# A fused recurrence and feed-forward kernel: spreading the first chunk's decays with four large matmuls per tile

## The chip, the cores and the metric

The kernel runs on one core of one Trainium2 chip. The metric is the device time of one execution in microseconds (us): the median of several runs. Engines are named as in the profile: PE (TensorE matmuls), PEld (its weight loads), DVE (VectorE), ACT (ScalarE), POOL (GpSimd), SP (SyncE, which issues all data transfers).

## What is computed

The reference, cut to what matters (B=4, H=8, S=768, D=40):

```python
for t in range(S):
    m_new = maximum(f[t] + m, i[t])
    f_stab, i_stab = exp(f[t] + m - m_new), exp(i[t] - m_new)
    C = f_stab * C + i_stab * outer(v[t], k[t])
    n = f_stab * n + i_stab * k[t]
    y[t] = sigmoid(o[t]) * (C @ q[t]) / maximum(abs(n @ q[t]), 1)
x = y.transpose(0, 2, 1, 3).reshape(B * S, H * D)        # 3072 x 320
h = x @ w_in                                             # 320 -> 2048
out = where(h > 0, h, exp(minimum(h, 0)) - 1) @ w_out    # 2048 -> 320
```

## The kernel before

**Tiles.** Time is cut into 6 chunks of 128 steps, and a tile is one chunk of one batch element with its 8 heads: 24 tiles, n = 4 x chunk + batch element. Inside a tile the recurrence is done in two halves of 64 steps: the state is carried from half to half, and within a half a 64x64 matrix per head holds the products of decays. The feed-forward part takes two tiles at a time (a block of 256 columns) and 16 slices of 128 of the 2048 inner features. While the weights are still arriving, the first blocks are done for some of the slices only, with partial sums stored and fetched back (`SPLITS`).

**Gates (`gate_chunk`, lines 355 to 392).** For each chunk the maximum m is a scan along time, the decays exp(f + m - m_new) go to `dec` (64 rows, one for each half, batch element and head, by 64 steps), and their running products to `cum`. Both are written to DRAM (`fstore`, line 381, and `bstore`, line 385).

**Decays spread over partitions.** A tile needs the decays of its 8 heads as rows that are the same on 64 partitions. `load` (line 394) fetches them back from DRAM with a source that repeats (`wdload` into `w`, line 416, and `bbload` into `bb`, line 425). For tiles 0 and 1 (`SPREAD_BY_PE`, line 181) PE does this instead: `spread` multiplies `dec` by one column of the identity, repeated 64 times, in 16 matmuls of 64 columns, and `spread_b` does the same for `cum` in 8. The result stays in PSUM, in the two banks `ph` for tile 0 and `pc` for tile 1, which the feed-forward part uses later.

**A tile's chain (`attention`, line 429).** On DVE the scan `ws` (line 478) turns the spread decays into the 64x64 matrices, and `kw` scales the keys by their last column. On PE come `kq` (line 496, products of keys and queries into the bank `pa`) and `us` (line 507, the sums for the state, also into `pa`). DVE multiplies `pa` into `w` (`wp`, line 522) and updates the state (`shrink`, `gather`). PE then forms the tile's output `y` in the bank `pb` (line 556): first state times queries (8 matmuls in the first chunk), then weights times values in 32 pieces, each 64 rows by 32 output partitions. DVE, ACT and POOL divide by the denominator and multiply by the gate (`den` to `result`), 64 columns are copied (`xdup`), PE transposes three blocks (`turn`, line 614, again into `pb`), and ACT and DVE split the result into a high and a low part (`xh`, `xl`), the feed-forward part's input. `pb` is one buffer, so the `y` of the next tile waits for `xl` of this one.

**Feed-forward (`ffn`).** Line 653 is the first layer (8 matmuls of 256 columns for one slice), lines 661 to 670 the nonlinearity and its split, line 680 the second layer (6 matmuls of 320 columns for one slice of a block).

**Weights (`conversion`, line 268).** They arrive as 64-bit words in 18 pieces (`wide`, line 285) and are turned into high and low parts by some eight steps on ACT, DVE and POOL.

**Order.** Every step is an `op` with a list of what it reads and writes. The table `PLACES` gives each step its place in one order of the whole program, and for some its engine (a letter behind the number). Each engine runs its steps in that order and waits for what a step needs; SP issues the transfers in that order too, and a transfer that must wait for its buffer holds those behind it.

Of the kernel before, what the change touches and what calls it, by code (L numbers as in the profile page):

```python
# [14 lines left out]
ALU = mybir.AluOpType  # L15
I32 = mybir.dt.int32
# [3 lines left out]
P = 128  # L20
# [6 lines left out]
    0 4 1 5 6v 3 35v 37 24 40 38 42 44 49 9 48 52 51 55 54 58 62 71 19 22 69 84 77 87 74 91 109 140 137 142 45 99  # L27
# [5 lines left out]
    775 2 10 14 17 13 21 20 15 23 26g 33 78 81 18 30a 12 11 8 39v 65 34 28 43 46 47 50 53 57 56 63 66 60 68v 70  # L33
    72g 76 80 85a 92 95 100 31 27 16 61 111 41 64 59 67g 83 88 94 96 93v 127 129 105 116 119 121g 124 126 128a 130
    133 138 7 25 29g 32 79 36 98 82 102 168g 170 173 178 143 145a 144 153 162 171 179 192 202 207 216 160 166 176
    183 222 228 233 241 245 256 262 251 255 90 86 89 75 73 101 97 135v 136 108 132 131 139 152g 151 146 149v 154
    158 161 163 165g 169 175 182a 184 187 191 113 114 112 107 110 115 117 164v 167 157 172 174 180 189g 185 190
    198v 227 197 210v 211 214 215 218 220a 221 224 226 229 235 243 247 257 264 277 283 307 260 266 274 278 285 298
    302 319 324 344 349 358 380 279 287 295 311 317 323 356 362 366 293 299 331 335 338 341 364 372 381 351 407
    412 365 411 527 330 340 360 363 382 398 406g 419 422 346 354 369 390 399 410 421 434 439 418 471 538 424 480  # L40
    615 203 193 181 188 186 199 195 246v 252 238 248 250 253 270 263 254v 267 291v 300 273 288 290 292g 294 297
    301a 305 310 313 236 232 217 208 213 237 240 296 303 281 286g 312 316 328 322 314 321 352 378 336 342v 343 345
    348 353 357a 361 371 375 122 194 209g 280 200 308 289 355 395 474 477 500 498 387 409a 396 402 428 430 433 438
    457 484 491 408 414 425 431 436 458 466g 497 502 445 449 465 469 473 481 499 512 517 462 467 476 511 516 521
    526 553 557 566 568 573 727 259 332 265 269 242 334 329 383 347 367 377g 389 393 417 403 397v 405 415v 446 429
    437 442 444g 447 448 451a 454 456 470 384 391 373 370 368 386 413 443v 435 427 440 455 459 460 463 452v 468
    478 513 472 486 488 492 494 496 508v 510 518 520 525 530 544 546 551 555 572 585 588 537 543 550 554 556 563
    569 594 602 560 564 587 591 599 605 610 619 623 570 576 596 601 606 612 629 646 652 667 767 670 832 607 614
    620 627 644 653 679 686 690 626 630 635 637 664 677 692g 707 714 658 663 689 693 695 698 713 756 760 671 680
    706 711 718 731g 753 780 785 748 805 836 781 813 815 722 729 737 740 759 774 779 819 828 735 741 757 758 764  # L50
    794g 798g 843 849 766 772 783 789 793 821 837 855 867 777 791 807 809 817 852 868 871 877 861 890 893 860 892
    990 799 804 847 851 876 880 885g 895 898 835 853 870 875 881 884v 888 903 910 883 886 889 899 901 908g 912g
    929 931 887 891 897 900 907 918v 920 934 938 894 942 944 902 949 1155 914 917 924 925 933 936 939g 964 986 922
    926 937 940 943 947v 950g 993 997 941 945 954 967 970 980 992g 1002 1023 951 958 965 969 987 1008 1016g 1031
    1042 1010 1045 1146 963 1047 1208 503 505 426 493 489 534 532 485v 487 539 545 547 549 613 583 577v 580 597v
    604 634 642v 647 649g 659 662 681a 684 687 691 595 593 581 584 524 598 542 632v 631 625 633 639 641 666g 669
    657v 674 676v 697 694 700 702 704 705 709 715a 721 725 728 376 450 475g 490g 464g 519 655 716 708 726 749 784
    788 734 736a 978 983 999 1003 1007 1012v 1026g 1049 1052 1006 1013 1018 1021 1024 1029g 1051 1055 1061 1017
    1019 1033 1038 1053 1057g 1060g 1067 1087 1036 1046 1054 1056 1059 1072g 1080 1092 1097 1062 1070 1078 1081
    1085 1094 1100g 1103 1107 1075 1083 1088 1091 1096 1099v 1108g 1120 1124 1101 1102 1104 1106 1109 1111 1114  # L60
    1132 1141 1110 1112 1116 1117 1119 1129g 1131g 1145 1153 1166 1168 1158 1372 611 617 540 578 574 603 645 683v
    682 621 660g 699 703 719g 733 710 723 730v 732 744 763v 768 769 770 773 787a 796 800 802 672 648 665 643 668
    717 678 738v 742 739 745 751 754 782 797 786v 790 792v 795 811 820 824 827 829 834 838a 841 845 848 1115 1118
    1122 1123 1125 1165v 1167 1174 1178 1126 1130 1135 1137 1140 1148 1157g 1181 1184 1156 1159 1171 1177 1180
    1183g 1185 1211 1219 1164 1169 1175 1179 1192 1196 1215 1223 1227 1187 1191 1201 1206 1225 1229v 1232g 1239
    1249 1205 1230 1234 1236 1238 1241g 1244g 1253 1255 1233 1237 1240 1242 1245 1247 1254 1264 1268 1243 1246
    1250 1252 1256 1258v 1259g 1270 1273 1279v 1303 1276 1446 724 720 712 762 765 801 803 778v 776 808 812 810 816
    846g 850 833 840 844 856 859 864 865 866 869 873 878 882 896 961 826 818 831 806 822 911 913 858v 906 854 857
    862 863 966 953 927 930 932v 956 974 979 981 982 984 985 988a 991 994 996 675 814 823 825g 872 830 904 874 935
    1063g 1065 1014 1011 1001 1004a 1257 1260 1262 1265 1267 1277v 1280g 1289 1292 1261 1269 1271 1272 1274 1278  # L70
    1284g 1306 1331 1275 1281 1285 1293 1295 1304 1316g 1333 1337 1283 1286 1290 1291 1296 1311 1335g 1347 1350
    1312 1319 1326 1329 1332 1336 1352 1376 1379 1325 1339 1344 1346 1349 1357 1367g 1393 1398 1343 1353 1355 1356
    1359 1377g 1382 1400 1403 1364 1369 1375 1378 1380 1391 1401 1407 1410 1434v 1455 1430v 1458 842 919 923 909
# [79 lines left out]
def tile_mlstm_then_elu_ffn(  # L153
# [634 lines left out]
```

## Time and profile before

| | before |
|---|---|
| median of 3 runs | 479.54 us (479.01 to 480.01) |
| the profiled execution's own time | 480.55 us |
| its span | 478.8 us |
| PE busy | 448.0 us, 94% of the span |
| DVE, ACT, POOL busy | 294.7, 229.0, 145.4 us |
| moved by DMA | 51.31 MB, 107 GB/s over the span |
| instructions that DMA brings in (queue q8) | 51 packets, 0.84 MB |

The span is the time between the first and the last instruction of the profiled execution; its own time is 1.75 us longer. Busy shares are sums over the whole span. Matmuls overlap, so PE's busy share says that it had something under way, not that it ran at its peak. In the trace, one float32 matmul of the program is two records on PE, a transpose or a float32r matmul is one.

### The profile page before, as it was taken

The page shows a single profiled execution, that of the slowest core. Times are in us where ns is not written, and L with a number is a line of the kernel's source. Part 1 is how long each engine was busy: PE and PEld are TensorE (multiplying, and loading weights), DVE is VectorE, ACT ScalarE, POOL GpSimd, SP SyncE. Part 2 cuts the span into 40 slices and gives each one's busy share as a digit, 9 for nine tenths or more (in the row PEclk, how much of TensorE's full clock was granted, in tenths as well). Part 3 has the DMA queues.
Part 4 walks back from the last instruction along what each step waited for, and adds up shares of the span by engine and source line. Part 5 has one row for each costly group of instructions (what it writes and reads, how often), then busy time and mean ns, then how long its engine had stood idle before and what let it go on. Part 6 is the DMA issues. An engine that isn't in the chain of part 4 may idle for free.

```text
span 478.8 us, 15219 instructions
## 1 busy us (share of the span) xinstructions
PE 448.0 (94%) x6574; PEld 435.6 (91%) x6574; DVE 294.7 (62%) x556; ACT 229.0 (48%) x440; POOL 145.4 (30%) x164
## 2 busy tenths in 40 slices
PE   4568999989799989999999999999999999999997
PEld 3557899979799989999999999999999999999996
DVE  6588899969959974767457425565663353353422
ACT  4466698669746432442533344333532334333443
POOL 2243235513432223433242543121223231222131
PEclk9998899989979999999999999999999999999999
DMA  7796967587944365620723304207050000010000
GB/s 220 174 256 186 249 189 194 128 231 197 258 111 114 95 162 125 171 77 15 168 65 98 107 2 129 85 12 207 0 137 7 0 16 1 1 44 1 27 1 27
DMA packets 23892, 51.31 MB, mean 107 GB/s; under 512 B 4794, under 2 KB 11130, under 8 KB 23826
## 3 DMA queue, kind: packets, MB, share of 16 engines
q1 hardware_dynamic: 23826, 50.35, 39.4%
q8 instruction: 51, 0.84, 0.8%
q14 instruction: 15, 0.12, 0.1%
HBM read 44.24 MB, written 6.09 MB: 105 GB/s over the span
## 4 chain that ended last, share of the span: by engine, by line
PE 84%; DMA 3%; issue 3%; DVE 2%; POOL 1%; ACT 1%; SPq 1%; POOLq 0%; DVEq 0%
PE ph L653 36%; PE pc L680 35%; PE pb L556 6%; PE pa L496 3%; PE pa L507 2%; DMA qk<-in_qk 2%; PE pb L614 2%; DMA wide<-in_w_in 1%; DVE vko L594 0%; POOL xf L199 0%; DVE xl L619 0%; SPq L416 0%; POOL qk L520 0%; DVE w L522 0%; POOL den L592 0%
## 5 line engine op out<-in xcount | busy, mean ns | idle before, releaser
L653 PE MATMUL ph<-xh,w 128*128 128x256 f32 x960 | 186.3, 286 | 0.6 <-ACT xh L617 0.6
L680 PE MATMUL pc<-w,gh 128*128 128x320 f32 x768 | 177.8, 319 | 0.3 <-issue 0.3
L653 PEld LDWEIGHTS ph<-xh,w 128*128 128x128 f32 x960 | 148.6, 191 | 1.6 <-ACT xh L617 1.0
L680 PEld LDWEIGHTS pc<-w,gh 128*128 128x128 f32 x768 | 130.2, 194 | 1.4 <-issue 0.4
L665 DVE SCALAR_TENSOR_TENSOR e<-e,ph 128x512 f32<-128x512 f32 (+1 forms) x97 | 65.3, 677 | 101.8 <-ACT e L663 99.7
L653 PE MATMUL ph<-xl,w 128*128 128x256 f32 x576 | 124.0, 284 | 0.2 <-DVE xl L619 0.2
L680 PE MATMUL pc<-w,gl 128*128 128x320 f32 x384 | 121.2, 316 | 0.0
L661 ACT ACTIVATE e<-ph 128x512 f32<-128x512 f32 (+1 forms) x97 | 57.4, 593 | 133.1 <-PE ph L653 103.1
L653 PEld LDWEIGHTS ph<-xl,w 128*128 128x128 f32 x576 | 96.4, 191 | 0.4 <-DVE xl L619 0.4
L670 POOL TENSOR_TENSOR gl<-e,gh 128x512 fp32r<-128x512 f32 (+1 forms) x44 | 57.6, 1309 | 124.0 <-ACT gh L199 70.4
L680 PEld LDWEIGHTS pc<-w,gl 128*128 128x128 f32 x384 | 74.4, 194 | 0.0
L663 ACT ACTIVATE e<-e 128x512 f32<-128x512 f32 (+1 forms) x97 | 60.3, 627 | 2.3
L322 POOL TENSOR_TENSOR narrow<-narrow,wide 128x512 int32<-128x512 int32 (+1 forms) x18 | 27.5, 1529 | 59.4 <-issue 14.9
L670 DVE TENSOR_TENSOR gl<-e,gh 128x512 fp32r<-128x512 f32 (+1 forms) x53 | 38.1, 720 | 11.1 <-PE pc L680 6.5
L199 ACT CAST gh<-e 128x512 fp32r<-128x512 f32 (+1 forms) x52 | 31.5, 607 | 19.0 <-DVE e L665 18.3
L199 POOL CAST gh<-e 128x512 fp32r<-128x512 f32 x20 | 13.7, 687 | 49.4 <-DVE e L665 49.4
L478 DVE TENSOR_TENSOR_SCAN w<-w,ones 128x512 f32<-128x512 f32 x22 | 27.1, 1234 | 0.7 <-DMA w<-f_d 0.7
L556 PE MATMUL pb<-va,w 64*32 64x41 f32 x1536 | 21.3, 207 | 3.9 <-issue 3.9
L617 ACT CAST xh<-pb 128x384 fp32r<-128x384 f32 x24 | 11.4, 475 | 25.6 <-PE pb L614 24.3
L507 PE MATMUL pa<-va,vko 64*64 64x41 f32 x704 | 17.9, 237 | 5.4 <-issue 4.8
L556 PEld LDWEIGHTS pb<-va,w 64*32 64x32 f32 x1536 | 18.1, 113 | 5.3 <-issue 4.1
L619 DVE TENSOR_TENSOR xl<-pb,xh 128x384 fp32r<-128x384 f32 x24 | 13.3, 554 | 15.1 <-ACT xh L617 15.1
(82 smaller groups left out, 428.5 us busy)
## 6 DMA issues: line engine op xcount, KB each, us to landing
vko<-in_vko SPq DMA_DIRECT2D x24, 480.0 KB, 5.1
qk<-in_qk SPq DMA_DIRECT2D x44, 192.0 KB, 5.3
w<-f_d SPq DMA_DIRECT2D x44, 128.0 KB, 4.2
wide<-in_w_out SPq DMA_DIRECT2D x8, 640.0 KB, 8.5
wide<-in_w_in SPq DMA_DIRECT2D x8, 512.0 KB, 5.1
bb<-b_d SPq DMA_DIRECT2D x41, 96.0 KB, 3.6
out<-os SPq DMA_DIRECT2D x24, 160.0 KB, 3.1
sum<-os SPq DMA_DIRECT2D x12, 160.0 KB, 4.6
```

What stands on the lines that cost most here:

```text
L199: nc.scalar.copy(o, i) if e == "ACT" else eng[e].tensor_copy(o, i)
L322: lambda e: nc.gpsimd.tensor_add(word, word, high if by_act else low),
L478: lambda e: nc.vector.tensor_tensor_scan(flat, src, ones.rearrange("p h t -> p (h t)"), 0.0, op0=ALU.mult, op1=ALU.add),
L496: nc.tensor.matmul(pp()[HALF[s], two, j, :], kt[rows, j, HALF[s]], qt[rows, j, HALF[s]], start=True, stop=True, skip_group_check=True)
L507: nc.tensor.matmul(us(s)[HALF[two], j, :], rows[HALF[s], at : at + Q], vn[HALF[s], h, :], start=True, stop=True, skip_group_check=True)
L556: nc.tensor.matmul(y[at, two, j, :], a, m, start=(at.start, two) not in begun, stop=False, skip_group_check=True)
L653: nc.tensor.matmul(h, a[g][:, cols], m, start=(i == 0), stop=(i == len(prods) - 1), skip_group_check=True)
L661: lambda e, h=h, ev=ev: nc.scalar.activation(ev, h, AF.Relu, scale=-1.0), KHP, (KE,))
L663: lambda e, ev=ev: nc.scalar.activation(ev, ev, AF.Exp, scale=-1.0), (), (KE,))
L665: lambda e, h=h, ev=ev: nc.vector.scalar_tensor_tensor(out=ev, in0=ev, scalar=-1.0, in1=h, op0=ALU.add, op1=ALU.max),
L670: lambda e, gh=gh, gl=gl, ev=ev: eng[e].tensor_sub(gl, ev, gh.bitcast(F32)),
L680: nc.tensor.matmul(pc[a][:, 0:DM], x[:, sl], bw[g][:, j, :], start=(f == f0 and part == 0), stop=(f == f1 - 1 and part == 2))
```

## The change

The first chunk's decays, all four tiles, are now spread by PE (`SPREAD_BY_PE = 4`).

- Four small masks (`pick`) are summed out of the identity on DVE at the start. With them, `blockf` and `blockb` write a block-diagonal copy of `dec` and of half of `cum` into the two buffers `e` of the feed-forward part (64x512 and 32x256).
- `spread` is then two matmuls of 512 columns per tile and `spread_b` two of 256. Tiles 0 and 2 use the banks `ph`, tiles 1 and 3 the banks `pc`. For tiles 2 and 3 the result of `spread_b` is copied to `bb` (`keep`).
- Chunk 0 is no longer stored to DRAM, and tiles 2 and 3 no longer load from there: 11 transfers fewer (three stores, four of 128 KB, two of 128 KB and two of 96 KB).
- In the first chunk, weights times values is done in 20 pieces: 12 of 64 rows by 64 output partitions and 8 of 64 by 32.
- Block 1 is planned together with block 0, and `PLACES` is a new table for the whole program. `ones` is now added on POOL. The branches for `XDUP = False` are not used.

```diff
-    SPREAD_BY_PE = 2
+    SPREAD_BY_PE = 4
+    WIDE = 4
+    XDUP = True
...
+        for x, (how, sizes) in views.items():
+            n, axes = (HH, AX.X) if x == "j" else (8, AX.XY if x == "ba" else AX.X)
+            op(f"zpick{x} 0", "DVE",
+               lambda e, x=x, n=n, v=corner.rearrange(how, **sizes), axes=axes: nc.vector.tensor_reduce(
+                   first[x][:, 0:n], v, op=ALU.add, axis=axes),
+               (("ident", 0),), (("pick", x),))
...
+        if c == 0:
+            op("blockf 0", "DVE POOL",
+               lambda e: eng[e].tensor_mul(
+                   es[0][0 : 2 * BH].rearrange("p (h t) -> p h t", t=Q),
+                   d.unsqueeze(1).to_broadcast([2 * BH, H, Q]),
+                   first["h"].unsqueeze(2).to_broadcast([2 * BH, H, Q])),
+               KD + (("pick", "h"),), (("e", 0),))
...
+        if (c + 1) * B > SPREAD_BY_PE:
+          op(f"fstore {c}", "SP",
...
             def spread(e):
-                for h in range(H):
-                    for x in range(2):
-                        nc.tensor.matmul(
-                            fw[HALF[x], h, :], chosen(x * BH + b * H + h), dec[g], start=True, stop=True)
+                for x in range(2):
+                    nc.tensor.matmul(
+                        spot[0][HALF[x]], first["xb"][:, x * B + b : x * B + b + 1].to_broadcast([2 * BH, Q]),
+                        es[0][0 : 2 * BH], start=True, stop=True)
...
+            wide = [(0, 0), (0, 1), (1, 0)] if n < WIDE and c == 0 else []
+            pieces = [(other, s, j, 0, Q) for other in range(2) for j in range(HH) for s in range(2) if (other, s) in wide]
+            pieces += [
+                (other, s, j, 32 * x, 32) for other in range(2) for j in range(HH) for x in range(2) for s in range(2)
+                if (other, s) not in wide
+            ]
+            for other, s, j, at, m in pieces:
+                two = s ^ other
+                h = two * HH + j
+                add(slice(Q * s + at, Q * s + at + m), two, j, w[HALF[s], h, at : at + m], vn[HALF[s], h, :])
...
-        while made <= kb:
+        while made <= kb or made < SPREAD_BY_PE // 2:
```

What the change moves is seen on three places. PE's first steps before (line 471 is `spread_b`, 465 `spread`, 496 `kq`, 507 `us`, 556 `y`, 614 `turn`):

```order
L471 MATMUL ph1_144<-cum0_99,ident_73 64x64 x8
L465 MATMUL ph0_143<-dec0_97,ident_73 64x64 x16
L465 MATMUL pc0_145<-dec0_97,ident_73 64x64 x16
L496 MATMUL pa_141<-qk0_84 64x64 x16
L507 MATMUL pa_141<-va0_82,vko0_101 64x41 x16
L556 MATMUL pb_142<-C0_78,qk0_84 64x41 x8
L556 MATMUL pb_142<-va0_82,w0_104 32x41 x32
L471 MATMUL pc1_146<-cum0_99,ident_73 64x64 x8
L496 MATMUL pa_141<-qk1_85 64x64 x16
L507 MATMUL pa_141<-va0_82,vko1_102 64x41 x16
L614 MATMUL pb_142<-ident_73,xf0_109 128x128 x3
```

and now (493 is `spread_b`, 487 `spread`, 527 `kq`, 538 `us`, 587 `y`, 651 `turn`):

```order
L493 MATMUL pc1_150<-e1_124,pickba_77 64x256 x2
L493 MATMUL ph1_148<-e1_124,pickba_77 64x256 x2
L487 MATMUL pc0_149<-e0_123,pickxb_75 64x512 x2
L487 MATMUL ph0_147<-e0_123,pickxb_75 64x512 x2
L527 MATMUL pa_145<-qk0_88 64x64 x16
L538 MATMUL pa_145<-va0_86,vko0_105 64x41 x16
L587 MATMUL pb_146<-C0_82,qk0_88 64x41 x8
L587 MATMUL pb_146<-va0_86,w0_108 64x41 x12
L587 MATMUL pb_146<-va0_86,w0_108 32x41 x8
L493 MATMUL ph1_148<-e1_124,pickba_77 64x256 x2
L527 MATMUL pa_145<-qk1_89 64x64 x16
L538 MATMUL pa_145<-va0_86,vko1_106 64x41 x16
```

Behind these stands tile 2's `spread` and only then the `turn` of tile 0; tile 3's two spreads stand in the same way between the `y` and the `turn` of tile 1. Tile 1's spreads, which stood partly behind `y` of tile 0, are now all ahead of it, and ahead of tile 0's own.

SP's transfers at the start before:

```order
L285 DMA wide0_90<-in_w_in 128x512
L363 DMA fi1_96<-in_gates 32x256
L408 DMA vko0_101<-in_vko 128x960
L285 DMA wide1_91<-in_w_in 128x512
L403 DMA qk0_84<-in_qk 48x1024
L403 DMA qk0_84<-in_qk 64x1024
```

and now:

```order
L288 DMA wide1_95<-in_w_in 128x512
L377 DMA fi1_100<-in_gates 32x256
L431 DMA qk0_88<-in_qk 64x1024
L431 DMA qk0_88<-in_qk 48x1024
L436 DMA vko0_105<-in_vko 128x960
L288 DMA wide0_94<-in_w_in 128x512
```

Tile 0's queries and keys now go out ahead of its values and of the second piece of weights.

SP's transfers around the store of chunk 2's decays (`f_d2`) before:

```order
L285 DMA wide2_92<-in_w_in 64x512
L693 DMA os0_126<-sum2_4_1131 128x320
L693 DMA os1_127<-sum3_4_1187 128x320
L408 DMA vko2_103<-in_vko 128x960
L381 DMA f_d2_131<-dec0_97 64x64
L285 DMA wide2_92<-in_w_in 64x512
L285 DMA wide0_90<-in_w_out 128x640
```

and now:

```order
L288 DMA wide2_96<-in_w_in 64x512 x2
L740 DMA sum0_8_1322<-os1_131 128x320
L377 DMA fi1_100<-in_gates 32x256
L409 DMA f_d2_135<-dec0_101 64x64
L730 DMA os0_130<-sum2_4_1041 128x320
L730 DMA os1_131<-sum3_4_1165 128x320
L288 DMA wide0_94<-in_w_out 128x640
```

Of the weight piece that is loaded in two halves (64x512), one half stood behind that store; now both stand ahead of it.

## Rows read from the trace of the kernel before

**Rows 1.** The page: PE's busy share and granted clock in 40 equal slices of the span.

```profile
PE   4568999989799989999999999999999999999997
...
PEclk9998899989979999999999999999999999999999
```

**Rows 2.** PE's timeline, 0 to 62 us: start, us, what [idle before <-releaser].

```profile
4.98 1.12 PE L471 MATMUL ph<-cum,ident 64*64 64x64 f32 x16 [0.79 <-DVE cum L377]
5.89 1.92 PE L465 MATMUL ph<-dec,ident 64*64 64x64 f32 x32
7.60 1.92 PE L465 MATMUL pc<-dec,ident 64*64 64x64 f32 x32
12.52 1.13 PE L496 MATMUL pa<-qk 40*64 40x64 f32 x32 [3.00 <-DMA qk<-in_qk]
13.42 1.04 PE L507 MATMUL pa<-va,vko 64*64 64x41 f32 x32
14.88 1.08 PE L556 MATMUL pb<-C,qk 40*64 40x41 f32 x16 [0.41 <-ACT C L199]
15.88 1.30 PE L556 MATMUL pb<-va,w 64*32 64x41 f32 x61
21.12 0.34 PE L556 MATMUL pb<-va,w 64*32 64x41 f32 x3 [3.94 <-issue]
...
24.11 0.90 PE L614 MATMUL pb<-ident,xf 128*128 128x128 f32 x3
26.49 1.08 PE L556 MATMUL pb<-C,qk 40*64 40x41 f32 x16 [1.47 <-DVE xl L619]
...
31.36 0.87 PE L614 MATMUL pb<-ident,xf 128*128 128x128 f32 x3 [2.55 <-DVE xf L600]
...
34.29 0.58 PE L653 MATMUL ph<-xh,w 128*128 128x256 f32 x1
...
38.00 0.66 PE L556 MATMUL pb<-C,qk 40*64 40x41 f32 x16
...
39.33 0.38 PE L653 MATMUL ph<-xh,w 128*128 128x256 f32 x1
...
52.19 0.39 PE L653 MATMUL ph<-xh,w 128*128 128x256 f32 x1 [0.57 <-ACT xh L617]
```

**Rows 3.** DMA queues, 18.7 to 21.2 us: instructions brought in.

```profile
q8 instruction: 1, 0.02, 2.7%
```

**Rows 4.** DVE's timeline, 0 to 62 us.

```profile
9.19 1.22 DVE L478 TENSOR_TENSOR_SCAN w<-ph,ones 128x512 f32<-128x512 f32 x1
...
14.06 0.68 DVE L306 SCALAR_TENSOR_TENSOR narrow<-narrow,wide 128x512 int32<-128x512 int32 x1
```

**Rows 5.** The chain that ended last, 0 to 65 us: start, us, what.

```profile
47.49 3.50 PE pc L680 x12
...
54.83 1.76 PE pc L680 x12
56.59 0.62 PE pa L496 x32
57.22 0.45 PE pa L507 x32
57.66 2.09 PE ph L653 x16
```

**Rows 6.** SP's waits: issue line, what it waited for: us in total, times, longest us.

```profile
SPq L381 <- DVE os L696: 6.9, 1, 6.9
```

**Rows 7.** The chain that ended last, 92 to 140 us.

```profile
96.22 4.62 DMA wide<-in_w_in
...
118.32 9.55 DMA qk<-in_qk
...
128.69 2.37 issue
```

**Rows 8.** PE's timeline, 75 to 105 us.

```profile
102.68 0.37 PE L614 MATMUL pb<-ident,xf 128*128 128x128 f32 x1 [2.27 <-DVE xf L199]
```

More of the change, by code (lines that the diff above doesn't have):

```diff
@@ L216, in tile_mlstm_then_elu_ffn @@
     ident = const.tile([P, P], F32, name="ident")
+    first = {x: const.tile([2 * BH, 8], F32, name=f"pick{x}") for x in ("h", "xb", "j", "ba")}
     zeros = const.tile([2 * BH, Q], F32, name="zeros")
@@ L443, in attention @@
         by_pe = n < SPREAD_BY_PE
-        spot = ph if n == 0 else pc
-        KSP = [tuple(("ph", x, i) for i in range(2)) if n == 0 else (("pc", x),) for x in range(2)]
+        spot = pc if n % 2 else ph
+        KSP = [(("pc", x),) if n % 2 else tuple(("ph", x, i) for i in range(2)) for x in range(2)]
+        kept = by_pe and n >= 2
         op(f"va {n}", "POOL DVE",
@@ L450, in attention @@
         op(f"og {n}", "ACT", lambda e: nc.scalar.activation(o, o, AF.Tanh, scale=0.5), (), (KO,))
[L452 to L455 removed]
         flat = w.rearrange("p h t -> p (h t)")
         if by_pe:
[L459 removed]
             fb = spot[1][:, 0 : HH * Q].rearrange("p (j t) -> p j t", t=Q)
             def spread(e):
[L463 to L466 removed]
+                for x in range(2):
+                    nc.tensor.matmul(
+                        spot[0][HALF[x]], first["xb"][:, x * B + b : x * B + b + 1].to_broadcast([2 * BH, Q]),
+                        es[0][0 : 2 * BH], start=True, stop=True)
             def spread_b(e):
[L469 to L475 removed]
+                for two in range(2):
+                    nc.tensor.matmul(
+                        spot[1][HALF[two], 0 : HH * Q],
+                        first["ba"][BH : 2 * BH, 2 * b + two : 2 * b + two + 1].to_broadcast([BH, Q]),
+                        es[1][BH : 2 * BH, 0 : HH * Q], start=True, stop=True)
+            op(f"spread {n}", "PE", spread, (("e", 0), ("pick", "xb")), KSP[0])
+            op(f"spreadb {n}", "PE", spread_b, (("e", 1), ("pick", "ba")), KSP[1])
+            if kept:
+                op(f"keep {n}", "ACT DVE",
+                   lambda e, fb=fb: copy(e, bb[0:R2, :, HALF[1]], fb[0:R2]), KSP[1], KB)
+                fb = bb[:, :, HALF[1]]
+                KFB = KB
+            else:
+                KFB = KSP[1]
         src = spot[0] if by_pe else flat
@@ L515, in attention @@
         if by_pe:
-            op(f"qb {n}", "DVE",
-               lambda e: nc.vector.tensor_mul(qt[0:R2, :, HALF[1]], fb[0:R2], qt[0:R2, :, HALF[1]]), KSP[1], KQ)
+            op(f"qb {n}", "POOL DVE" if kept else "DVE",
+               lambda e: eng[e].tensor_mul(qt[0:R2, :, HALF[1]], fb[0:R2], qt[0:R2, :, HALF[1]]), KFB, KQ)
         else:
@@ L603, in attention @@
            KY + (KO,), (KXF,))
-        op(f"xdup {n}", "POOL DVE ACT",
-           lambda e: copy(e, xf[:, H * D :], xf[:, 2 * P : H * D]), (), (KXF,))
+        if XDUP:
+            op(f"xdup {n}", "POOL DVE ACT",
+               lambda e: copy(e, xf[:, H * D :], xf[:, 2 * P : H * D]), (), (KXF,))
         kb, place = where[n]
@@ L613, in turn @@
             for t in range(3):
-                nc.tensor.transpose(tp[:, t, :], xf[:, t * P : (t + 1) * P], ident)
+                if t == 2 and not XDUP:
+                    for x in range(2):
+                        nc.tensor.transpose(tp[x * R : (x + 1) * R, t, :], xf[:, t * P : H * D], ident)
+                else:
+                    nc.tensor.transpose(tp[:, t, :], xf[:, t * P : (t + 1) * P], ident)
         op(f"turn {n}", "PE", turn, (KXF, ("ident", 0)), (("pb", 0),))
```

189 lines of the change are left out of this document (88 added, 101 removed), and 13 rows, old and new, of the table PLACES.

## Prediction

> **What bounds the kernel now.** I read the page first, then PE's timeline, then the chain of waits and the waits of SP. PE's share is 9 tenths or nearly so from the fifth slice on, and the slices of the first 50 us are the low ones [rows 1]. So time can be won in two ways: the start, until the feed-forward part keeps PE busy, and the few places behind it where PE stands still.
>
> In the start the reader should see a chain that is nearly serial [rows 2]. Tile 0's queries arrive at 12.52 (PE had waited 3.00 for them). Its pieces begin at 15.88 and end at 21.46, though 61 of the 64 records take 1.3 us. Then tail and `turn` (24.11), the split, tile 1's `y` (26.49), its `turn` (31.36), the first feed-forward matmul (34.29). Tiles 2 and 3 come between the first slices, and block 1 begins at 52.19. In all of this the 3.94 us at 21.12 is the one wait that no engine explains. At its end DMA brings in one packet of instructions [rows 3], and PE had by then run 16+32+32+32+32+16+61 = 221 records since 4.98. I read it as PE waiting for its own instructions.
>
> The clock matters too. [...] The granted clock dips there, in the page's fourth and fifth slices [rows 1]. Before 38.00 PE also runs at the lower level, though the page's clock row still shows 9 for the first slices: two slices (16 matmuls) take 3.71 us from 34.29 to 38.00 [rows 2] against 2.09 later [rows 5].
>
> **The change, step by step** (times in the profiled execution).
>
> *Spreads.* Before, 32 records of 64 columns take 1.71 us (5.89 to 7.60), `spread_b`'s 16 take 0.91 (4.98 to 5.89) [rows 2]. The large matmuls stream the same columns: 4 records of 512, and 4 of 256. At the same price per column a tile costs 1.71 + 0.91 = 2.62 as before. The lower bound is half of that, 1.31, as `kq`'s records of 64 columns pass in half the time (32 in 0.90, 12.52 to 13.42) [rows 2]. [...]
>
> *Ahead of tile 0.* Two tiles' spreads, 5.2 us, as before, but behind the block copies. `blockb` holds half the columns of a 512-column DVE step (0.68 [rows 4]), so at most 0.7; `blockf` on POOL is covered as long as it ends before the two `spread_b` do, 1.8 us later. 4.98 + 0.7 + 5.2 = 10.9. Scan 1.22 [rows 4], then two DVE steps of under 0.68: `us` at 13.3, before 13.42. The queries are loaded earlier, but are no longer what ends last. Five DVE steps now lie between `kw` and the pieces, at most 3.4 us, where 15.88 - 13.42 = 2.5 were used before: I put the pieces at 16.3, 0.4 later.
>
> *Pieces.* The old 61 records pass at 21 ns (1.30 / 61). The new 40 records are 24 of the wide kind and 16 narrow. Lower bound: all at 21, 0.8. Upper: all at the 62 ns of the records of state times queries, which use one half of the output partitions (16 in 1.0, 14.88 to 15.88) [rows 2]: 2.5. I take the middle by their place: 16 records alternate between opposite quarters of the array (31 ns, 0.5), 8 stay in one quarter (62 ns, 0.5), 16 narrow ones stay in the same 64 rows (twice 20 ns, 0.64): 1.64, dearer than the 1.3 before. At the higher clock the extra is half, 0.17.
>
> *The instruction wait.* With 16 records of spreads instead of 80 and 40 pieces for 64, tile 0's `y` ends after 136 records, not 224; the 221st now falls into tile 1's `y`. A packet as late as before (it ended the wait at 21.12) is then in time. So the 3.94 us goes; bounds 0 to 3.94.
>
> *To the first slice.* Tile 0's `y` ends at 16.3 + 1.64 = 17.9. Behind it now stand `spread_b`, `kq`, `us` and `spread`: 0.91 + 0.90 + 1.04 + 1.71 = 4.6, longer than the tail that they hide (21.46 to 24.11, 2.65), so `turn` is at 22.5. From `turn` to the next `y` 2.38 (24.11 to 26.49): tile 1's `y` at 24.9, 1.6 ahead. It takes 1.0 + 1.64, and 4.6 follow again: `turn` at 32.1, now 0.7 late, but with `kq` and `us` of tile 2 done. First slice at 32.1 + 2.4 = 34.5, where it was 34.29.
>
> *To block 1.* Two slices 3.71 (38.2), tile 2's `y` 1.33 + 0.17 (39.7; 38.00 to 39.33 [rows 2]), tail 2.65 beside `kq`, `us` (0.62 + 0.45 [rows 5]) and a slice (1.05): `turn` at 42.35. Split 2.38 beside a slice: `y` 44.7, 46.2; tail 2.65 beside two second-layer slices (1.76): `turn` 48.9, block 1 at 51.3. Tile 4's `kq` and `us` (1.07) are done by then; before they followed. Lead 52.19 - 51.3 + 1.07 = 2.0 us. It comes from the clock: with PE's idle time cut into pieces I let it stay up, where before it fell.
>
> *Middle.* At 102.68 a `turn` waits 2.27 us for DVE's copy [rows 8]; DVE stood behind a weight piece that came in 4.62 [rows 7], and that was issued late, behind the store of chunk 2, for which SP was held 6.9 us [rows 6]. Both halves of that piece now stand ahead of the store. I count the 2.27. The rest of the new order I count as nothing: about the same slices lie between a tile's steps, which hide them; without that cover each `y` would cost its tail of 2.65.
>
> *At nothing.* The masks (two before the gates arrive, two among the gate steps), the `keep` copies and `qb` on POOL, beside PE's 4.6 us or a slice. Eleven transfers less help SP and DMA, but what they fed is not what ends last. The first `relu` must wait for the last spread's read of `e`, and the first slices for the banks; both are free before 34.5.
>
> Sum: 480.55 - 2.0 - 2.3 = 476.2 for a profiled execution like this one. The median of the runs shown is 1.0 lower (479.54): **475.2 us**.
>
> **Rivals.**
> - *Faster: the clock rises in the start, or the spreads cost half.* Against the clock: PE ran from 4.98 to 9.52 unbroken and was still at the lower level at 34.29 [rows 2]. For it: the new stretch (5.7 to 10.9) is longer. Two later spreads at half save 2.6, the first two as much: 475.2 - 5.2 = 470; with the first slices at the higher clock (3.71 to 2.09) 468.4. [...]
> - *The lead is eaten.* The packet is late by as much as before (3.94, and 2.0 is all the lead there is), or the clock falls as at 47.49 (1.74 for the second layer alone). Then 475.2 + 2.0 = 477.2 to 475.2 + 3.9 = 479.1, and with all pieces at 62 ns, 0.9 each for two tiles, 480.9.
> - *Slower: the transfers bunch.* SP issues in order; two second-layer weight pieces still stand behind the store of chunk 2, and the new order puts loads of several tiles in one row. One bunch is priced at 118 to 131: queries under way for 9.55 us, then 2.37 more for instructions [rows 7], and at the lower clock after it 1.74 for two second-layer slices [rows 5], with the 0.6 that PE waited for the queries some 4.7. It decides where a tile's queries land later than the slices ahead of its `kq` last. One more bunch and the 2.3 not won: 475.2 + 2.3 + 4.7 = 482.2; with a spoiled start 484 to 486.
> - *The change doesn't do what it says:* only if DVE, not the spread, is what `us` waits for. Then the spreads of tiles 2 and 3 are 5.2 us of PE for two loads that were hidden; that is inside the lead eaten.
>
> **The numbers.** Forecast (471 to 478) 0.45, faster rival 0.15, lead eaten 0.15, slower 0.25. About 0.2% (0.96 us) can be told from no change: faster is below 478.6, slower above 480.5. Faster 0.45 + 0.15 + half of the lead eaten, 0.67; same 0.08; slower 0.25. The range leaves out the best end of the one rival and the worst of the other: 467.5 to 483; the forecast's own is 471 to 478.
>
> **What would show it.** `y` of tile 0 without a gap near 21 us and tile 1's by 25; spreads of some 1.7 and 0.9 us per tile; first slice near 34.5 and block 1 near 51; second-layer matmuls at 1.76 for twelve between 45 and 51; no `turn` that waits over 2 us for DVE near 100. Wrong would be: an issue wait of 3 us or more in tile 1's `y`, pieces over 2 us per tile, or a `kq` that waits for queries for longer than 2 us after 60 us.

## The result, and the profile after

Measured side by side, 13 runs each: before 479.55 us (473.9 to 482.2), after 481.72 (480.6 to 484.1). The ratio is 1.0063, 95% interval 1.0036 to 1.0091: **slower by 0.6%, some 3 us** (2.2 by the medians), where 475.2 was forecast, 0.9% faster. The ratio is that of the mean times (481.80 to 478.78), without the one slow run of before, 482.2. The profiled execution took 480.93, its span is 479.1; the two profiled executions differ by only 0.4 us, less than the medians. So no difference between the two traces is a cause until a run has shown it.

The page of the changed kernel, PE's share and the granted clock in 40 slices [rows 1], and from the view of the DMA queues the packets of instructions of the whole span (packets, MB):

```profile
PE   5888999998797899999999999999999999999996
...
PEclk9999999999997999999999999999999999999999
```

```profile
q8 instruction: 50, 0.82, 0.7%
```

PE's timeline of the start (start, us, what [idle before <-releaser]; `f32 x39` are 39 records), against [rows 2]:

```profile
15.56 2.48 PE L587 MATMUL pb<-va,w 64*64 64x41 f32 x39
...
22.63 0.90 PE L651 MATMUL pb<-ident,xf 128*128 128x128 f32 x3
24.93 0.76 PE L587 MATMUL pb<-C,qk 40*64 40x41 f32 x10 [1.40 <-ACT C L201]
...
32.60 0.90 PE L651 MATMUL pb<-ident,xf 128*128 128x128 f32 x3
...
34.90 0.58 PE L690 MATMUL ph<-xh,w 128*128 128x256 f32 x1
...
38.72 1.35 PE L587 MATMUL pb<-va,w 64*64 64x41 f32 x37
...
43.67 0.52 PE L651 MATMUL pb<-ident,xf 128*128 128x128 f32 x3 [1.38 <-DVE xf L632]
...
45.44 0.49 PE L587 MATMUL pb<-C,qk 40*64 40x41 f32 x10 [0.31 <-POOL C L565]
...
49.49 0.52 PE L651 MATMUL pb<-ident,xf 128*128 128x128 f32 x3 [0.28 <-DVE xf L632]
...
51.29 0.39 PE L690 MATMUL ph<-xh,w 128*128 128x256 f32 x1
...
57.68 0.81 PE L587 MATMUL pb<-va,w 64*32 64x41 f32 x64
```

and the end of tile 4's `y` before:

```profile
60.29 0.81 PE L556 MATMUL pb<-va,w 64*32 64x41 f32 x64
61.03 0.39 PE L653 MATMUL ph<-xh,w 128*128 128x256 f32 x1
```

In this execution the start is what was forecast. The wait near 21 us is gone, and the clock does not fall between 45 and 51 (granted 1.00; 0.50 in before from 44.80 to 51.63). At 61.03 us tile 4's `y` is done in both; PE has then run 85 first-layer matmuls and 24 second-layer ones, against 64 and 24 before: 21 x 0.119 = 2.5 us ahead.

That the clock stays up is not the kernel's doing alone. Six profiled executions have this start, with the first slice at 34.90 to 34.92 in each (the changed kernel, a_pickend, a_pickend_shift32, a_half_again, a_shift32_epad, a_wide2_epad, all described below). Their granted clock is full from 37.75, 38.99, 39.93, 47.75, 40.16 and 40.70 on (in the changed kernel a first-layer matmul comes every 0.21 us ahead of 37.75 and every 0.12 behind), and block 1 begins at 51.29, 51.80, 54.47, 53.37, 52.32 and 52.18. Six executions with the instructions of before (before and its five kernels with pads alone) have the full clock from 35.99 to 39.10, and begin block 1 between 49.63 and 53.31. PE's timeline of a_pickend_shift32, whose clock is halved from 46.76 to 53.59 us:

```profile
46.95 2.27 PE L591 MATMUL pb<-va,w 64*64 64x41 f32 x37
...
52.52 0.84 PE L655 MATMUL pb<-ident,xf 128*128 128x128 f32 x3
```

So the lead of the start belongs to this pair of executions. With the 1.07 us of tile 4's `kq` and `us`, which are done by then, the means of these executions put it at 0.1 us (51.63 + 1.07 - 52.57), or at 0.9 without the three that carry added matmuls.

In this pair the loss comes later. As an estimate, PE's remaining work priced at the periods of before puts the change 1.9 us ahead at 128 us, 2.8 behind at 172, and 0.7 ahead at 200, when before has had its own wait at 177. Some 1.1 more go between 200 us and the end. PE's waits from 60 to 172 us on the same timeline, all of 0.9 us or more:

```profile
71.58 0.49 PE L587 MATMUL pb<-va,w 64*32 64x41 f32 x28 [0.94 <-issue]
88.82 0.52 PE L651 MATMUL pb<-ident,xf 128*128 128x128 f32 x3 [1.00 <-DVE xf L632]
...
109.47 0.39 PE L690 MATMUL ph<-xh,w 128*128 128x256 f32 x1 [1.30 <-DVE e L702]
...
131.51 0.43 PE L538 MATMUL pa<-va,vko 64*64 64x41 f32 x11 [1.86 <-issue]
...
151.90 0.59 PE L527 MATMUL pa<-qk 40*64 40x64 f32 x11 [2.87 <-issue]
...
166.60 0.36 PE L538 MATMUL pa<-va,vko 64*64 64x41 f32 x9 [1.32 <-issue]
```

"issue" is the profile's name for idle time that nothing in it explains. The view of the DMA queues for 149 to 150 us, in the longest of these waits, has one packet of instructions under way, and for 149 to 152 us (the busy share of the DMA engines in 40 slices) hardly anything beside it from 149.6 to 151.6:

```profile
q8 instruction: 1, 0.02, 6.3%
```

```profile
DMA  6434930300000000000000000000000000035965
```

PE's clock is halved there (the view by stretches: stretch and its length, busy time of PE, PEld, DVE, ACT, POOL, then PEclk, 0.50, DMA share and GB/s):

```profile
150.39:157.20 6.81, 5.30 (x63) 5.23 (x64) 5.19 (x9) 1.51 (x3) 2.97 (x3) 0.50 0.35 101
```

Waits named "issue" behind 60 us add up to 8.2 us here and to 5.1 before. The 2.27 of [rows 8] is gone, but 1.00 at 88.82 and 1.30 at 109.47, both for DVE, have come.

### The profile page after: what moved, and what is told of

It is laid out like the page before. It is cut to its first block, busy times and chain, and to the rows that moved or that the text cites. A ratio compares the mean times of both kernels' runs of the same rounds, so it can differ in the third digit from the quotient of the medians.

```text
span 479.1 us, 14899 instructions
## 1 busy us (share of the span) xinstructions
PE 451.7 (94%) x6414; PEld 430.6 (90%) x6414; DVE 304.9 (64%) x570; ACT 224.5 (47%) x431; POOL 149.7 (31%) x167
## 4 chain that ended last, share of the span: by engine, by line
PE 69%; DVE 4%; issue 3%; ACT 1%; POOL 0%; DVEq 0%; POOLq 0%; ACTq 0%
PE ph L690 32%; PE pc L717 29%; PE pb L587 4%; PE pa L527 2%; PE pa L538 2%; PE pb L651 1%; DVE e L702 1%; DVE gl L707 1%; DVE w L509 0%; DVE vko L513 0%; DVE vko L626 0%; DVE w L339 0%; ACT e L700 0%; POOL C L565 0%; DVE va L477 0%
## 5 line engine op out<-in xcount | busy, mean ns | idle before, releaser
L717 PE MATMUL pc<-w,gh 128*128 128x320 f32 x768 | 172.1, 311 | 0.0
L717 PEld LDWEIGHTS pc<-w,gh 128*128 128x128 f32 x768 | 126.5, 188 | 0.5
L717 PE MATMUL pc<-w,gl 128*128 128x320 f32 x384 | 118.7, 309 | 0.4 <-DVE gl L707 0.4
L707 POOL TENSOR_TENSOR gl<-e,gh 128x512 fp32r<-128x512 f32 (+1 forms) x36 | 47.9, 1332 | 65.1 <-PE pc L717 29.4
L707 DVE TENSOR_TENSOR gl<-e,gh 128x512 fp32r<-128x512 f32 (+1 forms) x61 | 45.0, 739 | 12.2 <-POOL gh L201 3.8
L201 POOL CAST gh<-e 128x512 fp32r<-128x512 f32 (+1 forms) x27 | 19.3, 714 | 64.6 <-DVE e L702 62.2
L587 PE MATMUL pb<-va,w 64*32 64x41 f32 (+1 forms) x1440 | 25.3, 205 | 2.2 <-issue 2.2
L509 DVE TENSOR_TENSOR_SCAN w<-w,ones 128x512 f32<-128x512 f32 x20 | 24.5, 1228 | 2.7 <-DMA w<-f_d 2.7
L587 PEld LDWEIGHTS pb<-va,w 64*32 64x32 f32 (+1 forms) x1440 | 21.6, 112 | 3.7 <-issue 2.5
L527 PEld LDWEIGHTS pa<-qk 40*64 40x64 f32 x768 | 15.4, 145 | 8.4 <-issue 5.1
```

The source lines that it names most:

```text
L201: nc.scalar.copy(o, i) if e == "ACT" else eng[e].tensor_copy(o, i)
L509: lambda e: nc.vector.tensor_tensor_scan(flat, src, ones.rearrange("p h t -> p (h t)"), 0.0, op0=ALU.mult, op1=ALU.add),
L527: nc.tensor.matmul(pp()[HALF[s], two, j, :], kt[rows, j, HALF[s]], qt[rows, j, HALF[s]], start=True, stop=True, skip_group_check=True)
L587: nc.tensor.matmul(y[at, two, j, :], a, m, start=(at.start, two) not in begun, stop=False, skip_group_check=True)
L707: lambda e, gh=gh, gl=gl, ev=ev: eng[e].tensor_sub(gl, ev, gh.bitcast(F32)),
L717: nc.tensor.matmul(pc[a][:, 0:DM], x[:, sl], bw[g][:, j, :], start=(f == f0 and part == 0), stop=(f == f1 - 1 and part == 2))
```

## The experiments

Three theories to begin with. **Pieces:** the 40 pieces cost more than forecast (2.3 to 2.5 us at the low clock, 1.35 at the high one; the old 64 take 1.3 at the low clock [rows 2] and 0.81 at the high one, at 38.59 us) and eat the lead. **Order:** the new order behind the start is worse. **Instruction fetches:** PE waits for its own instructions, at places that depend on how many instructions stand ahead. They are counted in pairs, one matmul with its weight load. Two more came out of the first traces: **address** (the new selector tiles, the four masks `pick`, moved all later tiles by 128 bytes a partition), with **start** (something else in the new code) as its rival. Results of all runs; the periods are the mean distance of consecutive matmuls' starts, 200 to 478 us, and "issue" is the sum of PE's waits of that name behind 60 us, both of the one profiled execution. Each ratio is to runs of before on the same chip beside it, whose median lay between 478.5 and 479.6:

| run | median us | ratio to before (95%) | period of layer 1, 2 in ns | issue us |
|---|---|---|---|---|
| before | 479.55 | 1 | 119.0, 146.6 | 5.1 |
| after | 481.72 | 1.0063 (1.0036-1.0091) | 119.8, 146.8 | 8.2 |
| a_narrow | 482.57 | 1.0102 (1.0061-1.0144) | 119.8, 146.8 | 6.1 |
| b_wide | 477.69 | 0.9987 (0.9959-1.0015) | 119.0, 146.6 | 4.3 |
| h_startA_restB | 481.60 | 1.0093 (1.0057-1.0129) | 119.8, 146.7 | 5.2 |
| h_startB_restA | 477.42 | 0.9991 (0.9963-1.0020) | 119.0, 146.6 | 2.6 |
| a_pickend | 480.12 | 1.0035 (1.0002-1.0067) | 118.9, 146.6 | 6.9 |
| b_pad128 | 480.17 | 1.0035 (1.0005-1.0065) | 119.8, 146.7 | 5.0 |
| b_xpad | 477.03, one run | - | 119.0, 146.7 | 5.4 |
| b_epad | 475.60, one run | - | 118.6, 146.2 | 5.6 |
| b_ospad | 479.63, one run | - | 119.0, 146.6 | 5.3 |
| b_xepad | 479.13, one run | - | 119.8, 146.8 | 4.8 |
| a_pickend_shift64 | 483.44 | 1.0087 (1.0053-1.0120) | 119.0, 146.6 | 5.7 |
| a_pickend_shift32 | 477.01 | 0.9937 (0.9907-0.9967) | 119.0, 146.6 | 3.3 |
| a_half_again | 477.84 | 0.9965 (0.9936-0.9993) | 119.0, 146.6 | 2.9 |
| c_spread2 | 478.11 | 0.9969 (0.9946-0.9992) | 119.1, 146.6 | 2.8 |
| h_startB_restA_wide | 478.95 | 0.9989 (0.9963-1.0015) | 119.0, 146.6 | 4.3 |
| b_shift32 | 478.16 | 0.9997 (0.9968-1.0026) | 119.1, 146.6 | 4.2 |
| a_shift32_epad | 477.50 | 0.9971 (0.9935-1.0007) | 118.6, 146.3 | 5.0 |
| a_wide2_epad | 476.81 | 0.9970 (0.9935-1.0005) | 118.6, 146.3 | 6.0 |

### Pieces and order, one at a time

a_narrow is the changed kernel with the old pieces, b_wide before with the new ones (the loop over `pieces` as in the change):

```diff
-    WIDE = 4
+    WIDE = 0
```

```diff
+            wide = [(0, 0), (0, 1), (1, 0)] if n < 4 else []
```

> The changed kernel with weights x values of the first four tiles in 64 narrow pieces again (WIDE 0), all else and the order as it is. Theory of the pieces: 64 narrow ones take 1.27 us at the low clock and 0.75 at the high one, the 40 take 2.25 and 1.30; two tiles of each give back 2 x 1.0 + 2 x 0.55 = 3.1 us, the turn of tile 3 ends near 47 us instead of 49.9, and the whole takes about 478.6 us (ratio 0.998). Theory of the order behind the start: the later order takes the gain away, 481 to 482 us. Theory of instruction fetches: 96 more pairs of instructions shift the places where TensorE waits for a packet of instructions; the sum of such waits after 60 us (8.2 us in the changed kernel, 5.1 before) sets the time, anywhere from 477 to 483, with the start's gain on top of it.

> The kernel before with the 40 pieces for its first four tiles, nothing else changed. Theory of the pieces: 3.1 us slower, 482.7 (ratio 1.0065). Theory of the order: under 0.5 us, since what bounds the start before is the chain of DVE and ACT and not TensorE. Theory of instruction fetches: 96 pairs fewer shift the waits, 477 to 484, with the piece price on top.

The two hybrids change the table of places alone: rows up to `turn 3` from one kernel, the rest from the other.

> The changed kernel, its own order up to the turn of tile 3, and the order and engines of the kernel before from there on. Theory of the order: the lead of 1.3 us that the changed kernel has at 60 us is kept, about 478.3 us (ratio 0.997). Theory of the pieces: the rest of the order is worth nothing, 481 to 482. Theory of instruction fetches: the waits after 60 us lie elsewhere than in either kernel; the time is that of the kernel before less 1.3 plus the difference of their sums.

> The kernel before, its own order up to the turn of tile 3, and the order and engines of the changed kernel from there on. Theory of the order: 3 us slower than before, about 482.5 us (ratio 1.006 to 1.007). Theory of the pieces: as before, 479 to 480. Theory of instruction fetches: before plus the difference in the sum of instruction waits after 60 us, 477 to 483.

Neither theory fits all four. The one of the pieces wanted 478.6 for a_narrow and 482.7 for b_wide (482.57 and 477.69 came), the one of the order 478.3 and 482.5 for the hybrids (481.60 and 477.42 came). Whatever has the changed kernel's code and start is slower by 0.6 to 1.0%, whatever has before's is not; the order behind `turn 3` is worth nothing that these intervals can tell. The narrow pieces did not help, and PE's timeline of a_narrow shows what they cost:

```profile
23.10 0.45 PE L536 MATMUL pa<-va,vko 64*64 64x41 f32 x8 [2.79 <-issue]
...
36.51 0.31 PE L414 MATMUL pb<-ident,fi 32*128 32x32 f32 x1 [1.16 <-DVE xl L654]
```

With 24 pairs of instructions more by then, PE stands for 2.79 us in tile 1's `us`, a wait named "issue", and the step ahead of the first slice comes at 36.51 instead of 34.66. The dear pieces have no such wait there.

### The address

In these traces every kernel with the changed code has a first-layer period of 119.8 ns, every one with the code of before 119.0, to the end of the run, where no step of the change runs any more.

a_pickend allocates the selectors last, b_pad128 puts an unused tile of their size into before:

```diff
     ident = const.tile([P, P], F32, name="ident")
-    first = {x: const.tile([2 * BH, 8], F32, name=f"pick{x}") for x in ("h", "xb", "j", "ba")}
...
     oss = tiles("os", P, DM)
+    first = {x: const.tile([2 * BH, 8], F32, name=f"pick{x}") for x in ("h", "xb", "j", "ba")}
```

```diff
     ident = const.tile([P, P], F32, name="ident")
+    pad = const.tile([P, 32], F32, name="pad")
```

> The changed kernel with its four selector tiles (32 bytes a partition each) allocated behind all other tiles, so that every other tile lies at the address that it has in the kernel before; nothing else differs. Theory of the address: the selectors moved the x tiles by 128 bytes and each first-layer matmul now takes 119.8 ns instead of 118.9, each second-layer one 146.75 instead of 146.6: 1536 x 0.95 ns + 1152 x 0.17 ns = 1.7 us, which comes back; first-layer period 118.9, 480.0 us against 481.7 (ratio to before 1.003). Theory of the start: the longer period comes of something else in the new code; 119.8 ns again, no change (ratio 1.006 or more).

> The kernel before with one unused tile of 128 bytes a partition behind ident, so that all later tiles lie where the changed kernel has them; no instruction differs. Theory of the address: first-layer period 119.8 ns, 1.7 us slower, ratio 1.0035. Theory of the start: 118.9 ns and ratio 1.000.

Both came out as the theory of the address has it. Slices of the first layer in the chain that ended last, 254 to 264 us, the changed kernel, and a_pickend:

```profile
254.65 2.88 PE ph L690 x24
257.53 0.88 PE pc L717 x6
258.41 2.88 PE ph L690 x24
```

```profile
255.49 2.85 PE ph L690 x24
258.33 0.88 PE pc L717 x6
259.21 2.85 PE ph L690 x24
```

The same 24 matmuls take 0.03 us less. With the table's periods before rounding, 119.78 - 118.87 = 0.91 ns x 1536, and 0.21 x 1152 in the second layer: **1.6 us**, 0.34% of the run, and both ratios moved by 0.3 to 0.35%. The periods show it; the ratios alone would not, since the intervals of a_pickend and the changed kernel overlap. Which tile it is, by the same pad ahead of single groups and a second one behind them (for b_epad):

```diff
+    pad = const.tile([P, 32], F32, name="pad")
     es = tiles("e", P, 512)
     ghs = tiles("gh", P, 512, dt=F32R)
     gls = tiles("gl", P, 512, dt=F32R)
+    pad2 = const.tile([P, 32], F32, name="pad2")
```

> The kernel before with 128 bytes a partition ahead of the tiles xh and 128 behind xl, so that of the tiles that come in steps of 256 bytes only xh and xl change their place within it. If it is the stream of x that costs, first-layer period 119.8 ns and second-layer 146.6 as before; if another tile's address or the sum of them does it, 118.9.

> The kernel before with 128 bytes a partition ahead of e and 128 behind gl: e, gh and gl alone change their place within steps of 256 bytes; x stays. If the address of what ACT, DVE and POOL write between the layers (or that of the stationary gh, gl) slows the matmuls: first-layer period 119.8 ns; if it takes x and these together, or a tile further ahead, 118.9.

> The kernel before with 128 bytes ahead of the output tiles os, the last ones: os alone changes its place. x alone gave a first-layer period of 119.0 ns, e, gh and gl alone 118.6, all tiles together 119.8. If os does it: 119.8 ns. If it takes x and e, gh, gl together: 118.9.

> The kernel before with 128 bytes ahead of xh and 128 behind gl: x, e, gh and gl change their place together, os and all tiles ahead of x stay. If x and these together lengthen the matmuls: first-layer period 119.8 ns, second-layer 146.75. If not: 118.9, and it is a tile ahead of x that does it.

It takes x and e, gh, gl together: 119.8 when both move by 128 bytes, 119.0 for x alone, 118.6 for e, gh and gl alone, and os does nothing. Of the slices of before behind 200 us two thirds run at 118.6 and one third at 120.0. With x and these moved nearly all run at 119.9, with e, gh and gl alone nearly all at 118.5; with x alone they stay split, at 117.5 and 120.0. Why is open: no run here shows what PE waits for.

### The place of the packets

50 packets (0.82 MB, 16 KB each) bring 6414 matmuls and as many weight loads: as an estimate 257 instructions each, 128 pairs. By it 64 pairs more ahead of everything move every limit by half a packet, and 128 leave all where they were. The added matmuls have no use and run while PE idles; their results are never read. With 32 of them (64 in the other run):

```diff
-        op(f"iT {c}", "PE", lambda e: nc.tensor.transpose(turned, i, ident[:BH, :BH]),
+        op(f"iT {c}", "PE", lambda e: [
+               nc.tensor.matmul(
+                   turned[0:BH, 0:1], ident[0:BH, 0:BH], ident[0:BH, 0:1], start=True, stop=True)
+               for _ in range(32 if c == 0 else 0)
+           ] + [nc.tensor.transpose(turned, i, ident[:BH, :BH])],
```

> The changed kernel with the selectors behind, and 64 more small matmuls (32x32 by one column, results never used) ahead of the first transpose, while TensorE idles at 1.3 to 4.8 us: half a packet of instructions (128 pairs) more in the stream. Theory of instruction fetches: the places where TensorE stands for a packet move by half a packet out of the dense stretches near 131, 152 and 167 us or into others; the sum of the instruction waits after 60 us changes from about 8 us by 3 or more, and the time with it (475 to 484), at an unchanged start. Rival: the waits are set by DMA traffic or by the order and not by the place in the packet: same places in the program, same sum within 1.5 us, 480 us.

> As the run with 64 added matmuls, with 32: each of them makes two pairs of instructions, so the 64 were one whole packet, and left the waits for instructions at the same places of the program (at 134, 154 and 169 us); 32 are half a packet. They end by about 5 us, when the first transpose starts anyway, so the start is not delayed (first slice near 34.9 us, 38 with the 64). Theory of instruction fetches: with half a packet more the waits leave those three places; their sum after 60 us (7.7 us of instruction waits in the run with the selectors behind) changes by 3 us or more, and the fall of the clock behind the wait at 152 us goes. Rival (waits set by the order or by DMA): same places, sum within 1.5 us, time as with the selectors behind, ratio 1.003.

I had meant 64 as half a packet; each made two pairs (the trace counts 128 in 6.98 us), so it became the control with a whole one. The chain that ended last, 140 to 170 us, of the changed kernel, of the whole packet and of the half one:

```profile
147.19 1.35 PE pb L587 x96
148.53 0.49 PE pa L527 x19
149.02 2.87 issue
...
163.61 1.19 PE pb L587 x96
164.80 0.48 PE pa L538 x23
165.28 1.32 issue
```

```profile
152.64 1.35 PE pb L591 x96
153.99 0.49 PE pa L531 x19
154.48 2.23 issue
...
167.58 1.19 PE pb L591 x96
168.77 0.48 PE pa L542 x23
169.25 0.83 issue
```

```profile
151.72 0.95 PE pb L591 x51
152.67 0.36 issue
153.03 0.64 PE pb L591 x45
...
163.25 1.19 PE pb L591 x96
164.44 0.61 PE pa L542 x32
```

A whole packet leaves the waits at the same record: behind 19 of the 32 of `kq`, behind 23 of the 32 of `us`. Half a packet takes them away, and the one at 131; two others came, 1.92 at 89 and 1.06 at 236 us. There the small matmuls run fastest (96 + 19 pairs in 1.84 us, nearly a packet), and as I read it, what counts is whether the limit falls into the end of such a run or ahead of it. The sum of issue waits fell from 6.9 to 3.3 us, the ratio from 1.0035 to 0.9937. The added matmuls do not raise the clock earlier (full from 39.93 us, 38.99 without them), and the gain comes behind 60 us. The 64 also delayed the start by 3.0 us (first transpose behind the start at 37.70 for 34.66), and the median rose by 3.3, the ratio by 0.0052 or 2.5 us: this delay of the start reached the end, in full within what the intervals can tell. Slack behind it did not absorb it. No run gives a lead in the start alone.

> The kernel before with the same 32 added matmuls (64 pairs, half a packet) ahead of its first transpose; they end near 4.9 us and delay the first spread by 0.3 us at most. Theory of instruction fetches: the waits of 2.4 us at 131 and 1.8 us at 177 leave their places, as do the falls of the clock behind them, and others come; the time changes by 1 to 5 us to either side (474 to 484). If it gains 3 us as the changed kernel did, the packet's place hides what the change is worth, and the change stays behind; if it gains nothing or loses, the kernel before had by luck a better place. Rival (order, DMA): within 0.5 us.

> The same kernel as the one with the selectors behind and 32 added matmuls (0.9937 there), once more, since the run with pads around e, gh and gl on top came out at 0.997 and not at 0.992. If the half packet is worth what the first run showed: 0.991 to 0.997 again. If that run was lucky: 0.997 to 1.000, as the kernel with pads, and the change is then worth at most 0.3%.

Before neither gains nor loses by the half packet: its waits at 131 and 177 us left, a new one of 2.38 came at 61. So the loss by the place, 0.7 to 1.0% (1.0035 to 0.9965 and to 0.9937), stood on the changed kernel's side. Measured again, the gain held, though smaller.

### One part alone, and combinations

c_spread2 has the four large matmuls for tiles 0 and 1 alone, the selectors behind, and the order of before with the six new steps put in:

```diff
-    SPREAD_BY_PE = 4
-    WIDE = 4
+    SPREAD_BY_PE = 2
+    WIDE = 0
```

> One part of the change alone: tiles 0 and 1 spread in 4 large matmuls each from the block-diagonal copy (selectors behind the other tiles); tiles 2 and 3 through memory as before, the old 64 pieces, the order and engines of the kernel before with the six new steps put in. The spreads take 2.6 us of TensorE a tile in either form, so only the 80 pairs of instructions that go can gain. Theory of instruction fetches: the wait of 3.9 us near 18 us goes, the turn of tile 0 comes up to 3 us earlier, and what of it the wait for the x and w1 transfers leaves, 0 to 2 us, reaches the end: ratio 0.996 to 1.000, if the later waits stay. Rival (start bound by the chain over DVE, POOL and ACT): the turn of tile 0 within 1 us of before's, ratio 1.000, or above with DVE's added steps.

PE's timeline of c_spread2:

```profile
13.92 1.13 PE L525 MATMUL pa<-qk 40*64 40x64 f32 x32 [3.87 <-DMA qk<-in_qk]
...
21.58 1.13 PE L525 MATMUL pa<-qk 40*64 40x64 f32 x32 [1.93 <-DMA qk<-in_qk]
...
23.46 0.90 PE L649 MATMUL pb<-ident,xf 128*128 128x128 f32 x3
...
33.33 0.58 PE L688 MATMUL ph<-xh,w 128*128 128x256 f32 x1
```

The spreads take what they took (1.97 and 1.1 us), the wait of 3.94 is gone, half of it now waits for tile 1's queries, and the first slice is 0.96 us earlier than in [rows 2]. The kernel gains 0.3% with 80 pairs fewer. The 0.96 us of the start are 0.2%; its later waits fell too (2.8 us for 5.1), and no run separates the two.

Then three combinations: the hybrid with b_wide's pieces, the half packet with b_epad's pads, and `WIDE = 2` with these pads.

> The kernel before with the 40 pieces for the first four tiles, its own order up to the turn of tile 3, the changed kernel's order behind it. If the two parts add: 0.9987 x 0.9991, 0.998, near 478. Theory of instruction fetches: 96 pairs fewer shift the later waits; 474 to 481.

> The changed kernel with the selectors behind, the 32 added matmuls, and 128 bytes ahead of e and behind gl. Theory of the address: first-layer period 118.6 ns, second-layer 146.2, 0.3 ns x 1536 + 0.35 ns x 1152 = 0.9 us less than without the pads: ratio 0.992, 476 us. If the shorter period of that look was chance: 118.9 and 0.9937.

> The changed kernel with the selectors behind, 128 bytes ahead of e and behind gl, and the 40 pieces for tiles 0 and 1 alone (tiles 2 and 3 in 64); no added matmuls. Theory of the pieces: 0.55 us less for each of tiles 2 and 3, 1.1. Theory of the address: 0.9 less. Theory of instruction fetches: from tile 2 on there are 48 pairs more in the stream, 0.38 of a packet, so the waits at 131, 152 and 167 us move as with 64 pairs: 2 to 4 us less. If all three hold: 475 us, ratio 0.991. If only the first two: 478, 0.998.

The first adds up as expected and gains nothing that can be told. In the other two the periods fell as expected, to 118.6 and 146.3 ns, but the time did not follow: 0.997 for both, and the sums of issue waits stayed high: 5.0 us for a_shift32_epad, above the 3.3 and 2.9 without the pads, and 6.0 for a_wide2_epad, which has no run without them. 0.9 us is 0.2%, less than these intervals can tell. **Two kernels beat both:** the changed one with its selectors behind all other tiles and half a packet ahead (0.9937 and 0.9965 in two measurements), and c_spread2 (0.9969). Their intervals are clear of 1. These runs do not tell which of the two is faster.

## Why the prediction was wrong

Right, by its own steps: the spreads (1.97 and 1.1 us at the low clock, the next row 1.8 and 0.9 behind); tile 0's pieces begin at 15.5 (forecast 16.3) and end at 18.0 (17.9); the `turn`s stand at 22.63, 32.60, 43.67, 49.49 (22.5, 32.1, 42.35, 48.9), the first slice at 34.90 (34.5), block 1 at 51.29 (51.3). The instruction wait in tile 0's `y` went. The lead at block 1 is 52.19 - 51.29 + 1.07 = 2.0 as forecast. The agreement of these last steps is luck: they hang on the clock between 38 and 52 us, and with the same start block 1 begins as late as 54.47 in other executions. "I let it stay up" held in five of the six, but in all six the clock rose no earlier than 37.75, and in one not before 47.75.

Mis-sized: the **pieces**. 1.64 us was taken at the low clock, by reading 62 ns as a lone record's time; 39 of them take 2.48, 37 at the high clock 1.35. By single starts at the low clock (15.56 to 17.05), records that alternate between opposite quarters come every 53 ns, records in one quarter every 107. The 62 was already two at once: in the trace of before the records of state times queries start in pairs, one pair every 107 ns. From 15.43 to 17.97 the 40 take 2.5, 0.9 more than forecast for each of two tiles. `turn` 0 came in time all the same, since the pieces began 0.9 earlier; `turn` 1 is 0.5 late.

For the spreads, 2.62 us a tile, the price per column of before, was an estimate: the kernel before has no records of 512 columns, and [rows 2] does not tell this price from the lower bound, 1.31. The runs showed 2.67 from start to start in the first tile (0.91 from 5.47 to 6.38, 1.76 from 7.37 to 9.13).

Mis-sized too: the **middle**. "I count the 2.27": DVE's wait went from 102.68, but 1.00 at 88.82 and 1.30 at 109.47 came. Nothing was won.

What failed is one sentence, **"The rest of the new order I count as nothing"**, and the list of what costs nothing. Two costs lay in neither. The selectors, "at nothing", moved x and the tiles between the layers by 128 bytes: 1.6 us (0.34%). And the wait for instructions was followed in tile 0 and 1 only: taking 160 pairs out (96 records of spreads became 32, and 4 x 24 pieces went) moved every limit behind it, into three dense stretches near 131, 152 and 167 us (before waits near 131 and 177). Half a packet undoes that: 0.7 to 1.0%. [rows 7] shows 2.37 us of "issue" at 128.69 in before; I put it down to transfers that bunch, as part of the slower rival, and called it a wait for instructions, but did not ask where the new order would put such waits. With both undone the change gains 0.35 to 0.63% (1.7 to 3.0 us), against the 0.9% forecast. What is missing, 1.3 to 2.6 us, may be the middle's 2.3, or the start's 2.0, most of which other executions do not have; no run separates them.

None of the rivals is what happened. The slower one had 482.2, near the time, by another mechanism: no `kq` waits for its queries for 1 us behind 60 us. The clock stays low until 37.75 (37.98 before) and the spreads cost what they did, so the faster one is out. Of "the lead is eaten" one part came true, the price of the pieces (0.9 each for two tiles). The late packet did not; the falling clock did in one execution of six, and nothing here says how often it does in the runs that were only timed.

## What to carry to other kernels

Here 160 pairs of instructions less moved the waits for instructions to other places, and half a packet more moved them again, for 0.7 to 1.0% of the time. Before a change that adds or removes instructions is judged by a percent, run it with half a packet of idle instructions ahead, and the kernel before as well. A new tile goes behind the others, or the period of the longest loop is compared with that of before ahead of any explanation. A lead read from one pair of traces is checked on more executions where the clock has a part in it. A delay of 3.0 us in the serial start cost 2.5 to 3.3 at the end; it was the two side effects that turned this change's sign.

## What the runs showed of the hardware

- All waits named "issue" of 0.5 us or more behind 60 us, 58 in 20 profiled executions, end 1.2 to 1.6 us after a packet of instructions has landed, and at that time PE has run 59 to 87 matmuls more than 128 for each packet that came. They take up to 3.7 us (h_startA_restB at 135). Around the longest of the changed kernel the DMA engines are nearly idle, so this one is not a transfer that is crowded out.
- The granted clock is halved in 24 of these 58 waits or within 2 us behind them, for the most part in the longer ones: 150.39 to 157.20 us here, and before 130.1 to 137.0 and 177.9 to 181.3, behind the waits at 131.05 and 177.01. The wait's price is then about twice its length, as an estimate: behind the 2.87 us, 16 first-layer matmuls take 3.71 us at 153.41, where 1.91 is what 16 take at 157.56, and with the `kq`, `us` and `turn` beside them some 2.7 us are lost. The waits at 131 and 167 us of the changed kernel had no such fall, and the fall at 102.83 us of before followed a wait for DVE (2.27 us, to 102.68).
- 128 bytes of placement changed the period of a stream of 256-column matmuls between 118.6 (b_epad) and 119.8 ns (b_pad128, b_xepad), from 119.0 in before.
- 128 added records of one column took 6.98 us, 54.5 ns each at the low clock (a_pickend_shift64), as much as those of 64 columns (53). In the spreads no such price shows on top of the columns: four records of 512 columns in 1.76 us, 7.37 to 9.13, are 0.86 ns a column; 32 of 64 in 1.71 are 0.83.
